# Re-laying a planner's engine orders in a gated-attention plus maxout kernel: load pace, margins, row-tiled groups, head order and filler products

## The chip, the core and the metric

The kernel runs on one core of one Trainium2 chip. The metric is the device time of one execution in microseconds (us); the median of several executions counts. A core has five engines that each run their own instruction list strictly in order: PE (matrix products; its weight loads are shown apart as PEld), DVE, ACT, POOL (element-wise work) and SP, which here only issues the loads from memory. They meet through semaphores: an instruction whose input is not there yet holds up everything behind it on its engine.

## What is computed

For 4 batches and 8 heads of 768 tokens with 48 channels each, a recurrent state is decayed and updated per token, and the result goes through a maxout layer:

```python
for t in range(S):
    state = alpha[:, :, t, :, None] * state + np.einsum('bhd,bhe->bhde', k[:, :, t], v[:, :, t])
    y[:, :, t] = np.einsum('bhd,bhde->bhe', q[:, :, t], state)
...
h1 = x @ w1          # x: y of all heads side by side, 3072 tokens x 384
h2 = x @ w2          # 384 x 1024
g = np.maximum(h1, h2)
return (g @ w_out).astype(np.float32)
```

## The kernel before

**Units.** The tokens are cut into 12 units of 256 tokens (two chunks, a = 0 and 1, of 128). Unit u belongs to batch u % 4, so the state passes from unit u - 4 to unit u. Each unit has an attention part, `gla(u)`, and a maxout part, `moe(u)`.

**The attention part.** One load brings alpha (tile af), six bring k, q and v by chunk (kf, qf, vf). ACT takes the logarithm (lg, L372; two buffers). PE sums it over the tokens in row-tiled products (`e_cs`, L393, called cs below: 4 products that use 64 of the 128 rows each) and forms the decays (`e_de`, L384). ACT then takes three kinds of exponentials (em L403, in place L406, de L409). DVE makes qn (L421) and POOL kn (L418) and casts v to vc (L424). For each chunk PE transposes qn and kn (L435, called tp), DVE copies them out (qk, L437), PE forms k times v (kv, L459) and the scores (`e_p`, L481, called p: 8 products on 48 of 128 rows, in two row halves), DVE masks these (pt, L487), PE forms y from the scores and the carried state (L496 and L499), ACT copies y (yc, L507), PE transposes it (L513, called xt), and DVE copies it to tile xt (L515).

**The maxout part.** max(h1, h2) = h2 + relu(h1 - h2), so the kernel computes relu(x (w1 - w2)) w_out + x (w2 w_out). Four h groups per unit (L534, 6 products each; group f needs the weight quarter w12 number f, made by DVE at L326) are followed by relu (ACT L545, or DVE L542 for group 1) and 22 output products (L562, called o; part of them need w2o = w2 w_out, formed once at L340 to L363 from all the weight quarters). ACT copies the result (L568) and issues the store (L571).

**What sets the order.** Nothing is ordered by hand. Each piece of work is recorded by `Plan.add` with its engine, an assumed duration, an assumed latency until others may use its result (`lat`, else the table `LAT`), and a key. `Plan.schedule` then runs the recorded work through time on all engines at once: whenever an engine is free, the ready piece with the smallest key is taken. The instructions are put out in the order of the starts so found; only this order reaches the chip, and the assumed times do not. So a wrong assumed duration does not make anything slower by itself; it puts pieces into the in-order list of an engine ahead of, or behind, where they would fit. Keys: `gla(u)` has 10u and a little more, `moe(u)` has 10u + `KEY_M`, the preparation of the weights has `KEY_W12`, `KEY_W` and `KEY_WO`. Loads run on SP in the order in which they are recorded: those in the text `HEAD` first (u10 is alpha and chunk 0 of unit 1, u11 its chunk 1, w21 is quarter 1 of w2, and so on), then unit 2, 3 and so on. Input tiles have six buffers.

**Filler products.** `busy` (L351) records products on a zero tile that nobody reads: some with key -10 that stand first on PE, and some with key 1000, which the planner takes only where PE would have nothing else.

Of the kernel before, what the change touches and what calls it, by code (L numbers as in the profile page):

```python
# [13 lines left out]
class Op:  # L14
    __slots__ = ("n", "eng", "fn", "dur", "lat", "key", "deps", "succ", "start", "end", "ps", "w")

# [7 lines left out]
class Plan:  # L24
# [5 lines left out]

    LAT = {"PE": 0.21, "ACT": 0.15, "DVE": 0.14, "POOL": 0.14, "SP": 0.0}

    def __init__(self):
# [6 lines left out]

    def add(self, eng, fn, dur, reads=(), writes=(), key=0.0, lat=None, ps=()):
        o = Op(len(self.ops), eng, fn, dur, self.LAT[eng] if lat is None else lat, key)
        for r in reads:
            if r in self.last_w:
                o.deps.add(self.last_w[r])
            self.readers.setdefault(r, []).append(o.n)
        for w in writes:
            if w in self.last_w:
                o.deps.add(self.last_w[w])
            for r in self.readers.pop(w, ()):  # L50
                if r != o.n:
                    o.deps.add(r)
            self.last_w[w] = o.n
        for x in (*reads, *writes, *ps):
            if x in self.psum and x not in o.ps:
                o.ps.append(x)
                self.psum[x][2] += 1
        o.w = (*writes, *reads)[:1]
        self.ops.append(o)
        return o  # L60

    def schedule(self, caps):
        ops = self.ops
# [11 lines left out]
        free = {e: 0.0 for e in self.LAT}  # L75
# [28 lines left out]

        order, t, n_left = [], 0.0, len(ops)
        while n_left:
            moved = False
            for e in self.LAT:
# [3 lines left out]
                for n in ready[e]:  # L112
                    if ready_at[n] > t + 1e-9:
                        continue
                    o = ops[n]
                    k = (o.key, n)
                    if best is None or k < best[0]:
# [14 lines left out]
                free[e] = t + o.dur  # L132
                order.append(n)
# [25 lines left out]

KEY_W12 = 11  # L160
KEY_W = 12
KEY_WO = 13
KEY_M = 25
HEAD = "u00 u01 w20 w10 wo0 w21 w11 wo1 u10 w22 w12 wo2 u11 w23 w13 wo3"


@with_exitstack
def kernel(
# [18 lines left out]
    nc = tc.nc  # L187
# [106 lines left out]
    def load(u, part=None):  # L294
# [72 lines left out]
    def gla(u):  # L367
# [21 lines left out]
        def e_cs():  # L389
            for r in range(2):  # L390
                for a in range(2):
# [19 lines left out]
        for a in range(2):  # L411
# [65 lines left out]
            def e_p(qk=qk, pp=pp):  # L477
                for j in range(HP):
                    for e in range(2):
# [40 lines left out]
    def moe(u):  # L520
# [26 lines left out]
        for m in range(2):  # L547
# [51 lines left out]
    for u in range(NU):  # L599
        if u + 1 < NU:  # L600
            if u:
                load(u + 1)
            gla(u + 1)
        moe(u)
# [34 lines left out]
```

## Time and profile before

| what | value |
|---|---|
| three timed runs | 155.95, 157.93, 158.33 us; median 157.93 us |
| the profiled execution's own time | 157.39 us |
| its span (first to last instruction) | 155.5 us |
| busy on PE / DVE / ACT / POOL | 139.5 / 95.3 / 78.4 / 66.9 us |
| read from memory / written | 23.59 MB / 4.72 MB |
| first cs product on PE / last product ends | 5.36 us / 151.46 us |

Of the profile of an execution these views are used: the page with the span cut in 40 slices (a digit is the busy share in tenths; PEclk is the granted PE clock), the table of stages (busy time of each engine in a stretch that is chosen by its two times), the timeline of an engine (start, duration, line, output<-input, count, and in brackets how long the engine was idle before it and for what), and the chain of waits that ended last. PE overlaps the products, so the duration of a group of products by itself (some 0.2 to 0.3 us longer than its share) is less telling than the distance from one group's start to the next, or than the chain, which counts each stretch once.

### The profile page before, as it was taken

What the parts mean: (1) busy time and instruction counts of PE and PEld (TensorE: products, weight loads), DVE (VectorE), ACT (ScalarE), POOL (GpSimd) and SP (SyncE); (2) the same over time, 40 slices, a digit from 0 to 9 for tenths busy, and PEclk for the clock granted to TensorE, in tenths of its full rate; (3) what the DMA queues carried; (4) which work ended last, traced back from release to release, by engine and by line L of the source; (5) the groups of instructions that cost most, each with busy time, mean ns of one, the idle gap of its engine ahead of it and who ended that gap; (6) DMA issues with size and microseconds to landing.
All of it is one profiled execution on the core that took longest, in us unless ns stands there. A gap on an engine that the chain in (4) does not pass through costs nothing.

```text
span 155.5 us, 4176 instructions
## 1 busy us (share of the span) xinstructions
PE 139.5 (90%) x1642; PEld 99.0 (64%) x1642; DVE 95.3 (61%) x198; ACT 78.4 (50%) x164; POOL 66.9 (43%) x124
## 2 busy tenths in 40 slices
PE   7955895979999999999896969999999999999990
PEld 7843453556767676756664746766867667677750
DVE  6379627493889889496394476494681965931100
ACT  3603362338775672843925743744936537245430
POOL 7872223622736373471570671652734615500000
PEclk9998699699999999999999999999999999999998
DMA  4999999899999997998997999999911102002202
GB/s 118 221 274 325 278 250 259 254 289 203 239 221 255 232 265 157 287 212 181 267 239 152 188 276 184 294 226 198 261 27 68 40 0 101 4 0 101 100 6 101
DMA packets 94931, 28.58 MB, mean 184 GB/s; under 512 B 87744, under 2 KB 94912, under 8 KB 94912
## 3 DMA queue, kind: packets, MB, share of 16 engines
q1 hardware_dynamic: 91648, 23.60, 67.4%
q10 hardware_dynamic: 3264, 4.72, 8.4%
q8 instruction: 13, 0.21, 0.6%
q14 instruction: 6, 0.05, 0.1%
HBM read 23.59 MB, written 4.72 MB: 182 GB/s over the span
## 4 chain that ended last, share of the span: by engine, by line
SPq 39%; PE 29%; DMA 12%; ACT 6%; issue 4%; DVE 4%; POOL 2%; ACTq 1%; POOLq 0%; DVEq 0%
SPq L308 31%; PE pb L562 16%; DMA af<-in_alpha_dram 7%; SPq L322 6%; PE pb L534 5%; DMA vf<-in_v_dram 3%; PE pb L435 2%; DMA qf<-in_q_dram 2%; SPq L299 2%; ACT em L403 2%; PE pb L481 2%; DVE qn L421 2%; ACT os L568 2%; POOL kn L418 1%; PE pb L499 1%
## 5 line engine op out<-in xcount | busy, mean ns | idle before, releaser
L562 PE MATMUL pb<-wo,gt 128*128 128x384 f16 x192 | 39.9, 327 | 0.1
L534 PE MATMUL pb<-xt,w 128*128 128x256 f16 x288 | 36.0, 272 | 2.3 <-DVE w2T L345 2.1
L487 DVE TENSOR_TENSOR pt<-pb,u 128x512 f16<-128x512 f32 x48 | 30.3, 683 | 5.9 <-PE pb L481 5.6
L418 POOL TENSOR_TENSOR kn<-kf,em 128x384 f16<-128x384 f32 x24 | 23.5, 998 | 17.1 <-ACT em L403 7.6
L534 PEld LDWEIGHTS <-w 128*128 128x128 f16 x288 | 26.7, 97 | 5.8 <-DVE w L326 1.5
L545 ACT ACTIVATE gt<-pb 128x512 f16<-128x512 f32 x36 | 21.4, 598 | 12.9 <-PE pb L534 12.7
L424 POOL CAST vc<-vf 128x384 f16<-128x384 f32 x24 | 12.1, 504 | 33.4 <-DMA vf<-in_v_dram 16.6
L568 ACT COPY os<-pb 128x384 f32<-128x384 f32 x24 | 11.4, 477 | 25.4 <-PE pb L562 25.4
L421 DVE TENSOR_TENSOR qn<-qf,pb 128x384 f16<-128x384 f32 x24 | 12.5, 550 | 17.8 <-ACT pb L406 14.7
L451 POOL TENSOR_TENSOR sb<-tm,dd 64x192 f16<-64x192 f32 x40 | 20.1, 502 | 6.3 <-DVE tm L471 3.9
L562 PEld LDWEIGHTS <-gt 128*128 128x128 f16 x192 | 16.1, 98 | 8.4 <-DVE gt L542 0.5
L437 DVE COPY qk<-pb 128x1024 f16<-128x1024 f16 x24 | 16.0, 682 | 2.6 <-PE pb L435 2.2
L507 ACT CAST yc<-pb 128x384 f16<-128x384 f32 x24 | 11.4, 480 | 12.1 <-PE pb L499 12.1
L515 DVE COPY xt<-pb 128x384 f16<-128x384 f16 x24 | 8.5, 355 | 13.7 <-PE pb L513 8.4
L562 PE MATMUL pb<-w2o,xt 128*128 128x384 f16 x72 | 15.7, 327 | 0.0
L372 ACT ACTIVATE lg<-af 128x768 f16<-128x768 f32 x12 | 10.1, 841 | 9.8 <-DMA af<-in_alpha_dram 9.8
L542 DVE TENSOR_SCALAR gt<-pb 128x512 f16<-128x512 f32 x12 | 8.2, 686 | 10.0 <-PE pb L534 9.9
L481 PE MATMUL pb<-qk 48*128 48x128 f16 x192 | 10.0, 226 | 3.1 <-DVE qk L437 1.8
L403 ACT ACTIVATE em<-pb 128x384 f32<-128x384 f32 x24 | 11.3, 494 | 2.2 <-PE pb L384 1.0
L481 PEld LDWEIGHTS <-qk 48*128 48x128 f16 x192 | 5.7, 97 | 9.2 <-issue 4.3
L471 DVE TENSOR_TENSOR tm<-pb,sb 64x192 f32<-64x192 f32 x32 | 11.2, 351 | 0.6
L499 PE MATMUL pb<-vc,pt 128*128 128x48 f16 x192 | 11.5, 184 | 0.1
(51 smaller groups left out, 176.5 us busy)
## 6 DMA issues: line engine op xcount, KB each, us to landing
af<-in_alpha_dram SPq DMA_DIRECT2D x12, 384.0 KB, 5.1
kf<-in_k_dram SPq DMA_DIRECT2D x24, 192.0 KB, 4.5
qf<-in_q_dram SPq DMA_DIRECT2D x24, 192.0 KB, 4.5
vf<-in_v_dram SPq DMA_DIRECT2D x24, 192.0 KB, 4.4
out_dram<-os ACTq DMA_DIRECT2D x12, 384.0 KB, 3.2
w2f<-in_moe_w_dram SPq DMA_DIRECT2D x4, 384.0 KB, 4.5
w1f<-in_moe_w_dram SPq DMA_DIRECT2D x4, 384.0 KB, 4.8
wof<-in_moe_w_out_dram SPq DMA_DIRECT2D x4, 384.0 KB, 5.5
```

The source lines that it names most:

```text
L308: nc.sync.dma_start(out=T[n][:, a], in_=src[b, :, t0 + 128 * a : t0 + 128 * a + 128, :].rearrange("h p d -> p h d"),)
L403: add("ACT", lambda csv=csv, em=em: nc.scalar.activation(out=EM[em], in_=csv(), func=ACTF.Exp, scale=-1.0), 0.38, reads=[("cs", u, a)], wr ...
L418: add("POOL", lambda a=a, kn=kn, m3=m3: nc.gpsimd.tensor_mul(out=kn[:, :, 0:D], in0=KF[n][:, a], in1=EM[m3]), 0.95, reads=[("kf", n, a), ( ...
L421: add("DVE", lambda a=a, qn=qn: nc.vector.tensor_mul(out=qn[:, :, 0:D], in0=QF[n][:, a], in1=b32(("cs", u, a), DM).rearrange("p (h d) -> p ...
L437: add("DVE", lambda qk=qk, tp=tp: nc.vector.tensor_copy(out=qk, in_=b16(tp, 1024).rearrange("p (w j c) -> p w j c", w=2, j=HP)), 0.6, read ...
L451: add("POOL", lambda r=r, e=e, sb=sb, dd=dd, tmi=tmi: nc.gpsimd.tensor_mul(out=sb[r, :, e], in0=TM[tmi][r], in1=dd[r, :].unsqueeze(2).to_b ...
L481: nc.tensor.matmul(b32(pp[e], 512).rearrange("p (j c) -> p j c", j=HP)[:, j, :], lhsT=qk[r, 1, j, :], rhs=qk[r, 0, j, :], start=True, stop ...
L487: add("DVE", lambda e=e, pt=pt, pp=pp: nc.vector.tensor_mul(out=pt[:, e], in0=b32(pp[e], 512).rearrange("p (j c) -> p j c", j=HP), in1=u16 ...
L534: nc.tensor.matmul(t[:, m, :], lhsT=w12[:, ds, f * 128 : f * 128 + 128], rhs=xt[:, ds].rearrange("p a c -> p (a c)"), start=(ds == 0), sto ...
L545: add("ACT", lambda g2=g2, v2=v2: nc.scalar.activation(out=g2, in_=v2(), func=ACTF.Relu), 0.48, reads=[x], writes=[("gt", u % 3, f2)], key ...
L562: nc.tensor.matmul(b32(x, DM), lhsT=l, rhs=r, start=first and y == 0, stop=last and y == len(ws) - 1)
L568: add("ACT", lambda m=m, x=x: nc.scalar.copy(out=os_[:, m, :], in_=b32(x, DM)), 0.38, reads=[x], writes=[("os", u % 3)], key=k0 + 4 + m)
```

## The change

All edits are to what the planner assumes and to what is recorded; the instructions of the attention and maxout parts are the same, and only their order differs.

```diff
+    PAD = 0.15
+    SWITCH = 0.1
+    STICK = 2.0
...
-        o = Op(len(self.ops), eng, fn, dur, self.LAT[eng] if lat is None else lat, key)
+        o = Op(len(self.ops), eng, fn, dur, self.LAT[eng] + self.PAD if lat is None else lat, key)
+        o.tiled = tiled
...
-                    k = (o.key, n)
+                    k = (o.key - (self.STICK if o.tiled and was_tiled else 0.0), n)
...
+                if e == "PE":
+                    o.dur += self.SWITCH if was_tiled and not o.tiled else 0.0
+                    was_tiled = o.tiled
...
-KEY_W12 = 11
-KEY_W = 12
-KEY_WO = 13
-KEY_M = 25
-HEAD = "u00 u01 w20 w10 wo0 w21 w11 wo1 u10 w22 w12 wo2 u11 w23 w13 wo3"
+KEY_W12 = 5
+KEY_W = 6
+KEY_WO = 10
+KEY_M = 18
+NBUSY = 160
+HEAD = "u00 u01 w20 u10 w10 w21 u11 wo0 w23 wo1 w11 w22 wo3 w12 wo2 w13"
...
-            add("SP", l_a, 1.45, writes=[("af", n)], key=-1, lat=2.0)
+            add("SP", l_a, 1.5, writes=[("af", n)], key=-1, lat=2.5)
...
-                add("SP", l_c, 0.98, writes=[(nm, n, a)], key=-1, lat=2.0)
+                add("SP", l_c, 0.99, writes=[(nm, n, a)], key=-1, lat=2.5)
...
-        add("SP", lambda: nc.sync.dma_start(out=dst, in_=src), 1.1, writes=[(f"w{m}f", g)], key=-1, lat=2.0)
+        add("SP", lambda: nc.sync.dma_start(out=dst, in_=src), 1.2, writes=[(f"w{m}f", g)], key=-1, lat=2.5)
...
-        add("PE", e_cs, 0.42, reads=[("lg", lgi), "t2"], writes=[("cs", u, 0), ("cs", u, 1)], key=k0)
+        add("PE", e_cs, 0.35, reads=[("lg", lgi), "t2"], writes=[("cs", u, 0), ("cs", u, 1)], key=k0, tiled=True)
...
-            add("PE", e_p, 0.36, reads=[("qk", m3)], writes=pp, key=kk)
+            add("PE", e_p, 0.27, reads=[("qk", m3)], writes=pp, key=kk, tiled=True)
...
-            0.06, reads=[("os", u % 3)], key=k0 + 6, lat=3.0)
+            0.06, reads=[("os", u % 3)], writes=[("out", u)], key=k0 + 6, lat=2.0)
+        add("SP", lambda: None, 1.06, writes=[("out", u)], key=-2)
...
-    busy(30, -10)
-    busy(60, 1000)
+    busy(34, -10)
+    busy(NBUSY, 1000)
+    add("SP", lambda: None, 0.6, key=-3)
```

So the planner now takes 0.15 us more for every handoff, a little more for each load, and a stretch of 1.06 us on the load queue for every store (no instruction stands behind it: it only delays the assumed loads). After a row-tiled piece another row-tiled piece is preferred, and leaving one costs 0.1 us. The recorded filler products go from 90 to 194. Lines after the edits are 8 higher than in the listing of before (L351 is then L359, L534 is L542, L571 is L579).

Three places of the orders that follow. **ACT, middle of the kernel** (around unit 6; af_69 and lg_93 belong to unit 6, af_70 and lg_94 to unit 7, em_106 is written by the first exponential of unit 6 in the list, de_113 the last of unit 5). Before:

```order
L409 ACTIVATE de_113<-pb_62 128x16
L372 ACTIVATE lg_93<-af_69 128x8x2x48
L545 ACTIVATE gt_141<-pb_66 128x512
L545 ACTIVATE gt_141<-pb_64 128x512
L507 CAST yc_136<-pb_61 128x384
L568 COPY os_144<-pb_62 128x384
L507 CAST yc_135<-pb_61 128x384
L372 ACTIVATE lg_94<-af_70 128x8x2x48
L568 COPY os_144<-pb_68 128x384
L403 ACTIVATE em_106<-pb_61 128x384
```

Now, from the same de_113 on, first to the exponentials of unit 6:

```order
L417 ACTIVATE de_113<-pb_67 128x16
L380 ACTIVATE lg_93<-af_69 128x8x2x48
L576 COPY os_144<-pb_68 128x384
L579 DMA out_dram<-os_144 128x2x384
L553 ACTIVATE gt_142<-pb_64 128x512
L411 ACTIVATE em_106<-pb_68 128x384
```

and at the end of those exponentials:

```order
L515 CAST yc_136<-pb_67 128x384
L414 ACTIVATE pb_64<-pb_64 128x384
L417 ACTIVATE de_114<-pb_64 128x16
L380 ACTIVATE lg_94<-af_70 128x8x2x48
L576 COPY os_145<-pb_63 128x384
```

The logarithm of unit 7 stood ahead of the exponentials of unit 6; it now stands behind them. The logarithms of units 8 and 9 moved in the same way (unit 8's stands ahead of the small last exponential only).

**SP, the head.** From the last load of unit 0 on, before:

```order
L308 DMA vf_87<-in_v_dram 128x8x48
L322 DMA w2f_147<-in_moe_w_dram 128x3x256
L322 DMA w1f_148<-in_moe_w_dram 128x3x256
L322 DMA wof_149<-in_moe_w_out_dram 128x2x384
L322 DMA w2f_147<-in_moe_w_dram 128x3x256
L322 DMA w1f_148<-in_moe_w_dram 128x3x256
L322 DMA wof_149<-in_moe_w_out_dram 128x2x384
L299 DMA af_70<-in_alpha_dram 128x8x96
```

Now:

```order
L316 DMA vf_87<-in_v_dram 128x8x48
L330 DMA w2f_147<-in_moe_w_dram 128x3x256
L307 DMA af_70<-in_alpha_dram 128x8x96
L316 DMA kf_76<-in_k_dram 128x8x48
L316 DMA qf_82<-in_q_dram 128x8x48
L316 DMA vf_88<-in_v_dram 128x8x48
L330 DMA w1f_148<-in_moe_w_dram 128x3x256
L330 DMA w2f_147<-in_moe_w_dram 128x3x256
```

Unit 1 comes ahead of most weights. In both orders the head is 26 loads of the same sizes in all; the last is a quarter of w_out before and quarter 3 of w1 now, and from the 27th load on (alpha of unit 2) the queue is the same.

**PE, the row-tiled pieces in the middle.** qk are the operands of p, lg those of cs. Before, around the end of a p:

```order
L481 LDWEIGHTS qk0_129
L481 MATMUL pb2_63<-qk0_129 128x128
L481 LDWEIGHTS qk0_129
L481 MATMUL pb0_61<-qk0_129 128x128
L562 LDWEIGHTS xt0_137
L562 MATMUL pb6_67<-w2o0_154,xt0_137 128x384
```

Now, around the end of the second p of a unit:

```order
L489 LDWEIGHTS qk0_129
L489 MATMUL pb0_61<-qk0_129 128x128
L489 LDWEIGHTS qk0_129
L489 MATMUL pb6_67<-qk0_129 128x128
L401 LDWEIGHTS t20_157
L401 MATMUL pb7_68<-lg0_93,t20_157 128x384
```

In six units the second p is now followed by cs of the next unit, with no full-height product between. Counted over all of PE's list from cs of unit 2 to the end, a row-tiled piece is left for another kind 30 times before and 24 times now. Up to that same cs, PE's list has 24 h products, 12 o products, 28 y products and 9 xt products before; now 42, 8, 40 and 12. All products of w2o stand ahead of it in both; so does the attention of units 0 and 1, but for the y and xt of unit 1's second chunk, which before come behind it.

Fillers on PE: 45 ahead of cs of unit 0, 42 and 3 behind it before; 62 ahead of it, 96 between it and cs of unit 1, and 36 after that now, the last of them ahead of the first h product.

More of the change, by code (lines that the diff above doesn't have):

```diff
@@ L14 @@
 class Op:
-    __slots__ = ("n", "eng", "fn", "dur", "lat", "key", "deps", "succ", "start", "end", "ps", "w")
+    __slots__ = ("n", "eng", "fn", "dur", "lat", "key", "deps", "succ", "start", "end", "ps", "w", "tiled")
     def __init__(self, n, eng, fn, dur, lat, key):
@@ L39, in ps, with add @@
         self.psum[name] = [banks, group, 0, None]
-    def add(self, eng, fn, dur, reads=(), writes=(), key=0.0, lat=None, ps=()):
-        o = Op(len(self.ops), eng, fn, dur, self.LAT[eng] if lat is None else lat, key)
+    def add(self, eng, fn, dur, reads=(), writes=(), key=0.0, lat=None, ps=(), tiled=False):
+        o = Op(len(self.ops), eng, fn, dur, self.LAT[eng] + self.PAD if lat is None else lat, key)
+        o.tiled = tiled
         for r in reads:
@@ L103, in place @@
             return got
-        order, t, n_left = [], 0.0, len(ops)
+        order, t, n_left, was_tiled = [], 0.0, len(ops), False
         while n_left:
@@ L130, in schedule @@
                 ready[e].remove(n)
+                if e == "PE":
+                    o.dur += self.SWITCH if was_tiled and not o.tiled else 0.0
+                    was_tiled = o.tiled
                 o.start, o.end = t, t + o.dur
-                free[e] = t + o.dur
+                free[e] = o.end
                 order.append(n)
@@ L600 @@
         if u + 1 < NU:
-            if u:
+            if f"u{u + 1}0" not in HEAD:
                 load(u + 1)
```

## Prediction

> **What bounds the kernel now.** I read the page first, then the clock, then a table of stages, then the timelines of the engines around the holes that it shows.
>
> ```profile
> PE 139.5 (90%) x1642; PEld 99.0 (64%) x1642; DVE 95.3 (61%) x198; ACT 78.4 (50%) x164; POOL 66.9 (43%) x124
> PEclk9998699699999999999999999999999999999998
> DMA  4999999899999997998997999999911102002202
> ```
>
> PE is busy 90% of the span, but the load queue is full too until about slice 29 (113 us). The clock dips twice, near 16 and 28 us (rival 1). Which of PE and the loads rules is seen from stages that I cut at the start of cs of each unit; shown are those of units 4, 5, 6, 7, 8, 10 and 11, the last one up to the end of the last product. The columns are length, then busy time and instructions of PE, PEld, DVE, ACT, POOL, then granted clock, DMA share and GB/s. The last row sums all ten stages, from cs of unit 2 at 36.43 us on.
>
> ```profile
> 52.40:62.69 10.29, 10.29 (x147) 7.37 (x147) 8.75 (x19) 6.31 (x14) 5.75 (x11) 1.00 1.00 225
> 62.69:73.56 10.87, 10.58 (x134) 7.53 (x133) 7.70 (x16) 6.07 (x13) 5.67 (x11) 1.00 0.99 230
> 73.56:86.11 12.55, 10.70 (x129) 7.19 (x128) 7.13 (x15) 6.60 (x14) 5.38 (x11) 1.00 1.01 219
> 86.11:97.77 11.66, 10.36 (x130) 7.41 (x130) 7.28 (x16) 6.16 (x13) 5.87 (x12) 1.00 1.01 220
> 97.77:108.07 10.30, 10.13 (x126) 7.30 (x126) 6.61 (x13) 6.12 (x14) 5.53 (x11) 1.00 1.09 245
> 118.26:128.53 10.27, 10.12 (x125) 7.26 (x126) 6.46 (x13) 5.50 (x13) 4.27 (x8) 1.00 0.11 41
> 128.53:151.46 22.93, 22.80 (x218) 16.12 (x216) 8.44 (x17) 10.76 (x23) 4.27 (x8) 1.00 0.14 53
> sum 115.03, PE 111.05 PEld 78.39 DVE 72.75 ACT 64.14 POOL 50.17; mean PE 11.10 PEld 7.84 DVE 7.27 ACT 6.41 POOL 5.02
> ```
>
> From cs of unit 2 (36.43 us) to the last product (151.46 us) PE has 111.05 us of work in 115.03 us. So 3.98 us are holes, most of them between 73 and 98 us. A unit costs PE about 10.3 us. The loads are faster:
>
> ```profile
> 60.84 0.58 SPq L299 DMA_DIRECT2D af<-in_alpha_dram  x1
> 102.41 0.83 SPq L299 DMA_DIRECT2D af<-in_alpha_dram  x1
> ```
>
> These are the alpha loads of units 6 and 11: 41.57 us for five units, 8.3 us each. From unit 2 on the loads gain 2 us per unit on PE, so the end is set by PE: when it gets to cs of unit 2, how much work is then left, and the holes. What made the holes:
>
> ```profile
> 73.89 0.84 ACT L372 ACTIVATE lg<-af 128x768 f16<-128x768 f32 x1 [1.39 <-DMA af<-in_alpha_dram]
> 83.38 0.84 ACT L372 ACTIVATE lg<-af 128x768 f16<-128x768 f32 x1 [3.45 <-DMA af<-in_alpha_dram]
> 91.78 0.84 ACT L372 ACTIVATE lg<-af 128x768 f16<-128x768 f32 x1 [1.88 <-DMA af<-in_alpha_dram]
> ...
> 77.15 0.40 PE L435 MATMUL pb<-ident,qn 128*128 128x128 f16 x4 [0.53 <-DVE qn L421]
> 85.02 0.34 PE L513 MATMUL pb<-ident,yc 128*128 128x128 f16 x3 [1.19 <-ACT yc L507]
> 93.16 0.40 PE L481 MATMUL pb<-qk 48*128 48x128 f16 x8 [1.30 <-ACT gt L545]
> ```
>
> The logarithms of units 7, 8 and 9 stand so early in ACT's list that ACT waits for alpha, 1.39, 3.45 and 1.88 us, though their results are wanted only at cs of these units (86.11, 97.77, 108.07 us). What stands behind them (exponentials, yc, relu) is late, and PE waits 0.53 + 1.19 + 1.30 = 3.02 us of the 3.98.
>
> **Term 1, the middle: holes.** The planner now assumes later loads and counts the stores, and the logarithms of units 7 to 9 have moved behind the exponentials of the unit before. They will be reached some 4 us after cs of units 6, 7 and 8. Counted in the new list with the durations below, PE has 34, 44 and 55 us of work from cs of unit 2 (35 us) to these, so they start near 70, 80 and 91 us with a hole of about 1 us, so ACT asks for alpha at about 74, 84 and 95 us; the rows say that it landed at 73.9, 83.4 and 91.8. The waits of 1.4 to 3.5 us shrink to some tenths. What then comes late is little: 0.96 us of other holes stay. New ones can come near units 3 to 5, where the loads have hardly a lead and PE arrives earlier than before; I add 0.3. Holes: 1.3 us, at best 0.3 (the last two stages have 0.28 together), at worst the old 3.98.
>
> **Term 2, the head: when cs of unit 2 starts, and what is done by then.**
>
> ```profile
> 36.43 0.61 PE L393 MATMUL pb<-lg,t 64*128 64x384 f16 x4
> ...
> 32.32 0.83 POOL L330 CAST wo<-wof 128x768 f16<-128x768 f32 x1 [2.35 <-DMA wof<-in_moe_w_out_dram]
> ...
> 33.52 0.84 ACT L372 ACTIVATE lg<-af 128x768 f16<-128x768 f32 x1 [0.20 <-DMA af<-in_alpha_dram]
> ...
> 32.99 0.96 DVE L326 TENSOR_TENSOR w<-w1f,w2f 128x768 f16<-128x768 f32 x1
> ```
>
> The head loads the same 26 tiles in both orders, and its last one landed at 32.3 us (the POOL row had waited for it). Now w1's quarter 3 has that place: DVE makes w12 of it by 32.3 + 1.0 = 33.3. The one ahead, a quarter of w_out, lands about 1 us sooner; cast, it is ready at 32.1, and 12 products of w2o follow, 12 x 0.162 = 1.95 us: 34.1. Then the last h group of unit 0 (0.66), and cs of unit 2: 34.8, with handoffs 35.1 us. It cannot be before the logarithm of unit 2 is done, 33.52 + 0.84 = 34.4; as a late bound I take the 36.4 of now.
>
> PE has also done more by then: by the lists 18 h, 12 y and 3 xt products more, and 4 o products fewer. Durations of one come from the chain of waits, where the pieces stand back to back:
>
> ```profile
> 112.80 0.33 PE pb L481 x8
> 113.13 0.59 PE pb L562 x3
> ...
> 138.04 0.17 PE pb L513 x3
> ...
> 139.03 2.62 PE pb L534 x24
> 141.65 3.57 PE pb L562 x22
> ...
> 151.46 0.48 ACT os L568
> ```
>
> An h product is 2.62 / 24 = 0.109, an o product 3.57 / 22 = 0.162, an xt product 0.17 / 3 = 0.055 us; the 12 y products of a chunk took 0.37 us by their starts:
>
> ```profile
> 136.49 0.21 PE L496 MATMUL pb<-sb,qk 128*128 128x96 f16 x1
> ...
> 136.86 0.48 PE L562 MATMUL pb<-wo,gt 128*128 128x384 f16 x2
> ```
>
> So 18 x 0.109 + 0.37 + 3 x 0.055 - 4 x 0.162 = 1.85, rounded to 1.9 us, less is left behind cs of unit 2. That is possible since PE stood half empty there (two rows below), while the first h groups of unit 1 now fit in.
>
> **Term 3, row-tiled pieces.** Three o products right behind a p took 0.59 us instead of 3 x 0.162 = 0.49: leaving a row-tiled piece costs 0.10 us. It happens 24 times instead of 30 from cs of unit 2 on: 0.6 us less. Bounds 0 and 0.6.
>
> **Term 4, fillers, at nothing.**
>
> ```profile
> 1.05 4.29 PE L351 MATMUL pb<-wsrc 128*128 128x128 f16 x45 [1.05 <-DVE wsrc L250]
> 6.01 2.50 PE L351 MATMUL pb<-wsrc 128*128 128x128 f16 x42
> ```
>
> A filler takes 0.06 us, the first ones 0.095. 17 more ahead of cs of unit 0 push it back by 1.0 to 1.6 us (from 5.36), since they stand ahead in a strict list, and the next 48 push the transposes back by as much again. What hides it: nothing of unit 0 is wanted before the second quarter of w1 lands, about 26 us; PE's own rows show it waiting at 11 to 15 us. Were that cover gone, the 1.6 us would go onto cs of unit 2, which the bound of 36.4 holds. Margins and the stores' stretch on SP put out no instruction.
>
> **Sum.** 35.1 (cs of unit 2) + 111.05 - 1.9 - 0.6 = 108.55 of work + 1.3 of holes = 144.95, the last product. Behind it stand the copy, the store and its landing, 155.5 - 151.46 = 4.04, and outside the span 157.39 - 155.5 = 1.89. Together 150.9 us, against 157.39 of the profiled execution, which lies 0.5 under the median of the three runs (157.93; 155.95 to 158.33). I expect the new median at 150.9, 4.5% under the old one. With all best ends: 34.4 + 108.5 + 0.3 + 4.04 + 1.89 = 149.1.
>
> **Rival 1, the clock halves once more at a bad time.**
>
> ```profile
> 11.00:14.50 3.50, 2.00 (x29) 1.51 (x29) 3.26 (x8) 1.21 (x2) 0.88 (x3) 1.00 0.98 310
> 14.50:18.20 3.70, 3.20 (x21) 1.72 (x22) 3.46 (x6) 0.83 (x1) 1.26 (x2) 0.54 1.09 333
> ...
> 24.80:28.20 3.40, 1.42 (x19) 1.16 (x17) 3.20 (x6) 0.00 (x0) 1.66 (x2) 1.00 0.87 181
> 28.20:32.00 3.80, 3.80 (x27) 2.19 (x25) 1.78 (x4) 1.43 (x2) 1.63 (x4) 0.55 1.00 318
> ```
>
> Twice a stretch of 3.5 us with PE busy 57% and 42% is followed by as long a stretch at half clock. The new list has fillers until the first h group, about 19 us, and none after; from there to the second quarter of w1, about 27 us, PE has 6 us of work for 8. If that share again halves the clock, the stretch of 3.4 us would fall on 28 to 32 us or on 31 to 35, and at the worst half of it, 1.7 us, goes onto cs of unit 2: 152.6 us. Speaking against it is that 6 of 8 is more than either share in the rows. The Trainium skill (TensorE: Matmul & The Clock Gate, Part 1: The HAM clock gate) says that the clock falls to half after one idle window of about 3.4 us and rises after a busy one; the lengths agree with the trace (both slow stretches are about 3.4 us), but the rows show that half a window of idleness is enough. By that rule alone, with no window wholly idle, this rival would not occur.
>
> **Rival 2, the plan does not come true.** The margins are guesses, and if the logarithms still meet late loads (at 84 us the margin is only 0.5 us), the 3.98 us of holes stay: 35.1 + 108.55 + 3.98 + 4.04 + 1.89 = 153.6; with cs of unit 2 at 36.4 as well, 154.9. For it: ACT's list has its logarithms of units 3 to 5 as tightly as before. Against it: the lead of the loads grows by 2 us per unit.
>
> **Rival 3, slower: a handoff that is late in every unit.** In the new steady order y of the second chunk follows its p after cs, 12 h products, the first y and de: 0.43 + 0.10 + 1.31 + 0.37 + 0.2 = 2.4 us, in which DVE must mask both halves (2 x 0.64 us), with other copies queued ahead. If DVE is late, PE stands still with all its o products behind the waiting y. From 0.65 us per unit over the ten units left the gain is gone; at 1.0 us it is 150.9 + 10 = 160.9. For it: DVE is busy 8.75 of 10.29 us in the stage from 52.40. Against it: in the later stages DVE has 6.5 to 7.7 of 10.3, the same pieces per unit, and PE had no holes with 11 o products, y and 2 more between that p and its y: 11 x 0.162 + 0.37 + 0.32 = 2.5 us.
>
> **How the numbers follow.** Forecast 60%, rival 1 13%, rival 2 19%, rival 3 8%. About 2% is what a measurement of this kernel can tell from no change; 2% under 157.93 is 154.8. The forecast, rival 1 and half of rival 2 lie below: 82%. Half of rival 2 and a weak rival 3 are within: 12%. Slower by over 2%: 6%. The range runs from the best ends, 149.1 and a little for shorter handoffs, to the far end of rival 2: 148.8 to 155.0.
>
> **What would show it.** Right: cs of unit 2 near 35 us; the logarithms of units 7 to 9 wait under 1 us each; PE idle from there to its last product under 1.5 us; stages of 10.1 to 10.3 us from unit 4 on; one maxout part alone at the end, with no other change in the last 4 us. Wrong: alpha landing later than now (the load pace changed), a clock digit under 9 between 28 and 36 us (rival 1), ACT rows with waits for alpha of over 1 us (rival 2), or PE waiting for pt in each stage (rival 3).

## The result, and the profile after

The change takes 148.5 us in the median of four executions (147.72 to 149.33), the kernel before 157.4 us beside it on the same chip. The ratio is 0.946, with a 95% interval of 0.937 to 0.956: 5.4% faster. The forecast was 150.9 us (4.5% under its median of 157.93), its range 148.8 to 155.0. The direction is right. The median of 148.5 lies 0.3 us under the low end of that range, but the kernel before also ran 0.5 us faster here than in the three runs that the forecast started from; as a share, 5.4% lies between the 4.5% of the forecast and the 5.8% of its low end. Some executions of any kernel here are some per cent slower than the rest; ratios here and below leave out those over 1.5% above the fastest of their kernel.

The page of the profiled execution (149.33 us, span 147.3 us), the same three lines that were shown of before:

```profile
PE 139.4 (95%) x1746; PEld 105.7 (72%) x1746; DVE 96.2 (65%) x198; ACT 77.9 (53%) x164; POOL 66.8 (45%) x124
PEclk9999999599999999999999999999999999999999
DMA  4998969997999999969999999999999420030202
```

PE is busy for the same 139.4 us (before 139.5), 104 more filler products included, in a span that is 8.2 us shorter. One dip of the clock is left, in slice 8, near 27 us. The loads end in slice 32 (118 us).

The table of stages, cut at cs of a unit as before (the same columns; units 2, 4, 5, 6, 7, 8 and the last, then the sum of all ten):

```profile
37.70:45.26 7.56, 7.56 (x84) 4.78 (x85) 4.23 (x9) 4.81 (x11) 4.07 (x7) 1.00 1.08 243
...
53.67:64.37 10.70, 10.70 (x143) 7.87 (x141) 8.64 (x19) 6.61 (x15) 5.19 (x10) 1.00 0.93 208
64.37:72.09 7.72, 7.72 (x100) 5.33 (x100) 4.82 (x11) 4.88 (x11) 5.23 (x10) 1.00 0.99 210
72.09:82.00 9.91, 9.91 (x135) 7.49 (x130) 8.14 (x17) 5.85 (x13) 5.79 (x11) 1.00 1.02 225
82.00:92.28 10.28, 10.28 (x147) 7.93 (x142) 8.18 (x17) 5.98 (x14) 5.22 (x10) 1.00 1.01 229
92.28:102.02 9.74, 9.74 (x132) 7.39 (x127) 7.24 (x14) 5.95 (x14) 5.76 (x11) 1.00 1.06 243
...
121.12:143.31 22.19, 22.17 (x240) 16.14 (x234) 10.16 (x20) 10.39 (x22) 4.32 (x8) 1.00 0.11 39
sum 105.61, PE 105.59 PEld 77.72 DVE 71.89 ACT 61.57 POOL 50.12; mean PE 10.56 PEld 7.77 DVE 7.19 ACT 6.16 POOL 5.01
```

From cs of unit 2 on PE is busy for 105.59 of 105.61 us; it was 111.05 of 115.03. Two things are to be seen. The holes are gone altogether, as far as the profile shows idle time. And PE's *busy* time fell by 5.5 us, though the same instructions stand behind cs of unit 2 but for some 1.9 us of them: busy time is not work.

**What busy time hides.** I therefore took every product of PE from cs of unit 2 on, the distance from its start to the start of the next one, and compared it with the median distance of its kind in the kernel before (0.109 us for h, 0.162 for o, 0.056 for a transpose, and so on). What a distance has over its median is put down to the place where it stands.

| us, from cs of unit 2 to the last product's end | before | change |
|---|---|---|
| all products at the median distance of their kind | 104.0 | 102.2 |
| over it, at the steps where a wait is shown (shown as idle) | 5.7 (3.9) | 0 (0) |
| over it, at the edges of row-tiled pieces | 6.4 | 5.1 |
| over it, at the edges of other pieces | 0.3 | 0.2 |
| inside a piece (negative, since the four cs products lie two by two) | -1.4 | -1.9 |
| sum | 115.0 | 105.6 |

So the 9.4 us are 1.8 of work done earlier, 5.7 of holes, 1.3 at row-tiled edges and 0.6 in the two last rows. Before had 11 steps with a shown wait; each lasted 0.16 us (1.8 / 11) longer than is shown as idle, since the profile's end of the product ahead, which is modelled, lies that much inside the wait. Against the 9.4 stands cs of unit 2, at 37.70 us instead of 36.43.

**ACT in the middle.** The logarithms of units 6, 7 and 8 in ACT's timeline, and the issue of alpha of unit 7 in SP's:

```profile
69.30 0.84 ACT L380 ACTIVATE lg<-af 128x768 f16<-128x768 f32 x1 [1.85 <-DMA af<-in_alpha_dram]
77.72 0.84 ACT L380 ACTIVATE lg<-af 128x768 f16<-128x768 f32 x1 [1.44 <-DMA af<-in_alpha_dram]
86.11 0.84 ACT L380 ACTIVATE lg<-af 128x768 f16<-128x768 f32 x1
```

```profile
72.70 1.58 SPq L307 DMA_DIRECT2D af<-in_alpha_dram  x1
```

ACT still stands 1.85 and 1.44 us for alpha of units 6 and 7, and alpha of unit 7 came at 77.7 us instead of 73.9, its issue at 72.70 instead of 68.52. But PE shows no idle time for it: there is other work in its list just then.

**The head.** Three timelines (POOL, DVE, PE) around cs of unit 2, and the stretches in front of it by windows:

```profile
33.63 0.83 POOL L338 CAST wo<-wof 128x768 f16<-128x768 f32 x1 [2.61 <-DMA wof<-in_moe_w_out_dram]
```

```profile
34.60 0.96 DVE L334 TENSOR_TENSOR w<-w1f,w2f 128x768 f16<-128x768 f32 x1
```

```profile
35.00 2.11 PE L367 MATMUL pb<-wo,w2T 128*128 128x384 f16 x12
36.95 0.82 PE L542 MATMUL pb<-xt,w 128*128 128x256 f16 x6
37.70 0.50 PE L401 MATMUL pb<-lg,t 64*128 64x384 f16 x4
```

```profile
22.09:25.50 3.41, 2.04 (x37) 1.52 (x38) 3.38 (x8) 0.67 (x2) 2.27 (x4) 1.00 0.95 320
25.50:28.91 3.41, 3.41 (x19) 2.13 (x18) 2.32 (x6) 0.54 (x1) 0.83 (x1) 0.50 0.96 311
...
25.37:37.70 12.33, 12.33 (x102) 8.69 (x100) 7.42 (x12) 5.52 (x10) 2.48 (x3) 0.86 0.96 283
```

The last quarter of w_out landed at 33.63 us and was cast by 34.46 (the prediction had it landed near 31.3 and cast by 32.1); the last quarter of w12 was made from 34.60 to 35.56. The order of pieces in front of cs is the predicted one (12 products of w2o, the last h group, cs), 2.6 us later. But PE did not wait for these weights. It has no gap from 25.37 us on, and by the distances its pieces from there to 37.70 are 10.5 us at their medians; 1.7 us more lie in the window of 3.41 us that ran at half clock, and 0.2 at edges. It came to the 12 products at 35.00 straight from 18 h products. Ahead of 25.37 us PE waits for DVE (four waits of 0.25 to 0.53 us from 22 us on), which is busy for 3.38 of the 3.41 us of the window from 22.09.

**The end.** The chain of waits ends with one maxout part alone:

```profile
137.10 2.62 PE pb L542 x24
139.72 3.59 PE pb L570 x22
```

Before it ended with two of them, one behind the other; the second stands in the last two rows here, the first in the prediction's rows from 139.03 us on:

```profile
145.22 2.62 PE pb L534 x24
147.84 3.59 PE pb L562 x22
```

This moves work, and does not save any: from the last product to the end of the span it is 4.0 us in both.

### The profile page after: what moved, and what is told of

The parts are those of the page before. It is cut to its first block, busy times and chain, and to the rows that moved or that the text cites. A ratio compares the mean times of both kernels' runs of the same rounds, so it can differ in the third digit from the quotient of the medians.

```text
span 147.3 us, 4387 instructions
## 1 busy us (share of the span) xinstructions
PE 139.4 (95%) x1746; PEld 105.7 (72%) x1746; DVE 96.2 (65%) x198; ACT 77.9 (53%) x164; POOL 66.8 (45%) x124
## 4 chain that ended last, share of the span: by engine, by line
PE 81%; SPq 8%; DMA 4%; DVE 3%; issue 1%; ACT 0%
PE pb L570 30%; PE pb L542 23%; SPq L316 7%; PE pb L443 6%; PE pb L489 5%; DMA w1f<-in_moe_w_dram 4%; PE pb L367 3%; PE pb L507 3%; PE pb L521 3%; PE pb L401 3%; PE pb L504 2%; PE pb L467 2%; PE pb L392 2%; DVE qk L445 1%; DVE pt L495 1%
## 5 line engine op out<-in xcount | busy, mean ns | idle before, releaser
L570 PE MATMUL pb<-wo,gt 128*128 128x384 f16 x192 | 38.6, 328 | 0.0
L542 PE MATMUL pb<-xt,w 128*128 128x256 f16 x288 | 37.3, 273 | 1.3 <-DVE w L334 1.3
L542 PEld LDWEIGHTS <-w 128*128 128x128 f16 x288 | 25.9, 98 | 7.3 <-issue 1.9
L570 PEld LDWEIGHTS <-gt 128*128 128x128 f16 x192 | 17.1, 98 | 8.4
L445 DVE COPY qk<-pb 128x1024 f16<-128x1024 f16 x24 | 16.6, 690 | 9.6 <-PE pb L443 7.4
L429 DVE TENSOR_TENSOR qn<-qf,pb 128x384 f16<-128x384 f32 x24 | 13.0, 551 | 14.3 <-ACT de L417 5.0
L359 PE MATMUL pb<-wsrc 128*128 128x128 f16 x194 | 14.5, 237 | 1.1 <-DVE wsrc L258 1.1
L380 ACT ACTIVATE lg<-af 128x768 f16<-128x768 f32 x12 | 10.1, 842 | 8.3 <-DMA af<-in_alpha_dram 8.1
L359 PEld LDWEIGHTS <-wsrc 128*128 128x128 f16 x194 | 13.0, 108 | 1.3 <-DVE wsrc L258 1.1
L414 ACT ACTIVATE pb<-pb 128x384 f32<-128x384 f32 x24 | 11.5, 499 | 0.0
```

The source lines that it names most:

```text
L359: add("PE", lambda: nc.tensor.matmul(bank("wq0")[:, 384:512], lhsT=wsrc[:, 0:128], rhs=wsrc[:, 0:128], start=True, stop=True), 0.107 if ke ...
L429: add("DVE", lambda a=a, qn=qn: nc.vector.tensor_mul(out=qn[:, :, 0:D], in0=QF[n][:, a], in1=b32(("cs", u, a), DM).rearrange("p (h d) -> p ...
L445: add("DVE", lambda qk=qk, tp=tp: nc.vector.tensor_copy(out=qk, in_=b16(tp, 1024).rearrange("p (w j c) -> p w j c", w=2, j=HP)), 0.6, read ...
L542: nc.tensor.matmul(t[:, m, :], lhsT=w12[:, ds, f * 128 : f * 128 + 128], rhs=xt[:, ds].rearrange("p a c -> p (a c)"), start=(ds == 0), sto ...
L570: nc.tensor.matmul(b32(x, DM), lhsT=l, rhs=r, start=first and y == 0, stop=last and y == len(ws) - 1)
```

## The experiments

Theory, as it stood ahead of the runs: the gain is the holes of the middle, which the logarithms standing too early on ACT made, and it comes with the assumed pace of the loads; the keys and the head only do their small part. Rivals: the head order and the keys carry it; or the margins do; or the row-tiled preference. "Vs before" and "vs change" say which kernel was edited. All of them compute the whole result.

| run | ratio to before (95%) | cs of unit 2 | from there to the end of the last product | idle shown in it | over, at waits | over, row-tiled |
|---|---|---|---|---|---|---|
| before | 1 | 36.43 | 115.0 | 3.94 | 5.7 | 6.4 |
| the change | 0.946 (0.937–0.956) | 37.70 | 105.6 | 0.00 | 0 | 5.1 |
| e1_pace | 0.970 (0.962–0.978) | 38.76 | 108.4 | 0.29 | 1.1 | 5.8 |
| e2_ln_late | 0.998 (0.993–1.004) | 35.52 | 116.2 | 4.97 | 6.7 | 6.5 |
| e3_no_pace | 0.966 (0.957–0.975) | 36.70 | 108.8 | 1.99 | 3.0 | 4.7 |
| e4_fill90 | 0.944 (0.935–0.953) | 37.02 | 105.5 | 0.00 | 0 | 5.1 |
| e5_no_pad | 0.959 (0.953–0.964) | 38.24 | 106.6 | 0.05 | 0.2 | 5.6 |
| e6_no_tiled | 0.949 (0.938–0.961) | 37.40 | 106.8 | 0.46 | 1.0 | 5.1 |
| e7_head | 0.986 (0.978–0.995) | 37.31 | 112.0 | 2.03 | 4.0 | 6.0 |
| e8_no_keys | 0.961 (0.953–0.969) | 38.27 | 107.5 | 1.29 | 2.0 | 5.1 |
| e9_ln_behind_relu | 0.988 (0.982–0.995) | 36.76 | 113.4 | 2.13 | 3.9 | 6.5 |
| e10_pace_pad | 0.965 (0.958–0.972) | 36.47 | 108.5 | 0.49 | 0.8 | 6.2 |
| e11_paired_p | 0.951 (0.943–0.959) | 37.50 | 105.8 | 0.45 | 1.1 | 4.3 |
| e12_pad_double | 0.963 (0.956–0.971) | 37.08 | 108.0 | 1.87 | 2.2 | 4.9 |

Columns three to seven are us of one profiled execution each, the last two by the distances between starts. The ratio of each run is to the kernel before timed beside it.

**e1_pace** (vs before): the load pace alone.

```diff
-            add("SP", l_a, 1.45, writes=[("af", n)], key=-1, lat=2.0)
+            add("SP", l_a, 1.5, writes=[("af", n)], key=-1, lat=2.5)
...
-            0.06, reads=[("os", u % 3)], key=k0 + 6, lat=3.0)
+            0.06, reads=[("os", u % 3)], writes=[("out", u)], key=k0 + 6, lat=2.0)
+        add("SP", lambda: None, 1.06, writes=[("out", u)], key=-2)
...
+    add("SP", lambda: None, 0.6, key=-3)
```

The other loads go to 0.99 and 1.2 us, 2.5 us of latency, as in the change.

> The kernel before with one thing of the change: the assumed load pace (1.5, 0.99 and 1.2 us, latency 2.5), the 0.6 us at the start of SP and the stretch of 1.06 us per store. In its list the logarithms of units 7 to 9 stand behind the exponentials of the unit before, as in the change; keys, head, margins, row-tiled preference and fillers are as before. Theory (the holes between 73 and 98 us came from logarithms that stood too early, and the pace alone moves them): the 3 us of shown holes go, ratio to before 0.975 to 0.982, and PE's shown waits from cs of unit 2 on fall from 3.9 us to under 1. Rival (the margins at handoffs and the new head are what removed the waits): ratio 0.99 to 1.00, other waits of 2 to 4 us in their place.

Measured: 3.0% faster. Its stages of units 6 and 7, and the sum, in the table of stages:

```profile
73.70:84.40 10.70, 10.52 (x131) 7.39 (x132) 7.43 (x16) 6.02 (x14) 5.77 (x11) 1.00 1.09 244
84.40:94.40 10.00, 10.00 (x125) 7.13 (x124) 7.08 (x15) 5.86 (x13) 5.18 (x10) 1.00 1.02 226
...
sum 108.41, PE 108.12 PEld 78.17 DVE 71.72 ACT 62.86 POOL 49.42; mean PE 10.81 PEld 7.82 DVE 7.17 ACT 6.29 POOL 4.94
```

These two stages took 12.55 and 11.66 us before. A few assumed durations that no instruction carries give more than half of the whole gain. Most of the edit is the stretch for the store: by the old numbers the planner loads a unit in 1.45 + 6 x 0.98 = 7.3 us, by the new ones in 1.5 + 6 x 0.99 + 1.06 = 8.5, and the chip took 8.3 (alpha to alpha, before).

**e2_ln_late** (vs before): the logarithms of units 7 to 9 moved on ACT behind the last exponential of the unit before, nothing else.

```diff
+    lns = [o for o in P.ops if o.eng == "ACT" and o.w[0][0] == "lg"]
+    des = [o for o in P.ops if o.eng == "ACT" and o.w[0][0] == "de"]
+    for u in (7, 8, 9):
+        lns[u].start = max(lns[u].start, des[u - 1].start + 1e-6)
```

> The kernel before with its order kept, but for three instructions: the logarithms of units 7, 8 and 9 are moved on ACT behind the last exponential of the unit before. Theory (they block ACT while alpha is not there): 3 us less, ratio 0.978 to 0.983, and no wait of ACT for alpha of over 1 us from 70 us on. Rival (ACT would have been late anyway, or the wait reappears in qn, kn or vc, which wait for their own loads): ratio 0.99 to 1.00.

Measured: no difference. PE's and ACT's timelines, and two stages:

```profile
79.80 0.33 PE L459 MATMUL pb<-vc,kn 128*128 128x96 f16 x4 [0.66 <-ACT gt L545]
...
90.88 0.33 PE L459 MATMUL pb<-vc,kn 128*128 128x96 f16 x4 [0.61 <-ACT gt L545]
```

```profile
78.42 0.83 ACT L372 ACTIVATE lg<-af 128x768 f16<-128x768 f32 x1
79.16 0.59 ACT L545 ACTIVATE gt<-pb 128x512 f16<-128x512 f32 x1
```

```profile
51.60:63.76 12.16, 10.46 (x147) 7.30 (x147) 8.79 (x19) 6.32 (x14) 5.78 (x11) 1.00 0.93 207
...
75.22:86.24 11.02, 10.36 (x129) 7.28 (x129) 7.30 (x15) 6.16 (x13) 5.25 (x10) 1.00 0.96 215
```

The logarithm now waits for nothing (78.42), but the relu that stands behind it (79.16) is what PE's next piece wants: PE waits 0.66 us at 79.80. The stage of unit 6 fell from 12.55 to 11.02 us, and the three stages that the edit touches are 33.2 us together instead of 34.5. Others grew in this execution: that of unit 4 is 12.16 instead of 10.29, with 1.7 us of holes, in which DVE waited 1.85 us for a load of q; all lists up to there are those of before, so the edit did not make this hole. One profiled execution can therefore not tell the three stages' 1.3 us from chance; the median of the executions, which shows no gain, is what counts. So the theory in its simple form, "the place of three logarithms", is not borne out.

**e9_ln_behind_relu** (vs before): the same three behind two more relus.

```diff
+    gts = sorted(o.start for o in P.ops if o.eng == "ACT" and o.w[0][0] == "gt")
+    for u in (7, 8, 9):
+        lns[u].start = [s for s in gts if s > des[u - 1].start][1] + 1e-6
```

> As e2_ln_late, but the logarithms of units 7 to 9 go one step further back on ACT, behind the two relu pieces that follow the last exponential; nothing else of the order before is touched. Theory (the early logarithms did cause the holes of 73 to 98 us, and e2 only put 0.8 us of logarithm ahead of the relu that frees the bank for the second kv): those stages fall to 10.3 to 10.6 us each, ratio to before 0.978 to 0.986. Rival (each place in that list has some piece that is late, so single moves gain nothing; the whole list must be laid anew): 0.992 to 1.00, with waits of 0.5 us and more at another place in each unit.

Measured: 1.2% faster, between what the theory and its rival gave. The stages of units 6, 7 and 8, and ACT's timeline:

```profile
74.44:85.20 10.76, 10.45 (x129) 7.27 (x129) 7.23 (x15) 6.16 (x13) 5.24 (x10) 1.00 0.99 220
85.20:95.49 10.29, 10.29 (x130) 7.32 (x130) 7.21 (x16) 6.17 (x13) 5.66 (x11) 1.00 1.04 233
95.49:106.77 11.28, 10.41 (x125) 7.30 (x125) 6.72 (x13) 6.95 (x15) 5.64 (x11) 1.00 0.98 222
```

```profile
99.60 0.84 ACT L372 ACTIVATE lg<-af 128x768 f16<-128x768 f32 x1 [0.76 <-DMA af<-in_alpha_dram]
```

Units 6 and 7 gain 12.55 + 11.66 - 10.76 - 10.29 = 3.2 us, close to the 3.0 that the prediction read from the rows. In the next stage 0.98 us (11.28 for 10.30) goes back: ACT now asks for the next alpha too early (0.76 us), and PE waits 0.67 us for the relu behind it. Moved by hand, a wait goes on to the next unit; laid anew as a whole (e1) it does not.

**e3_no_pace** (vs change): the reverse of e1.

> The change with the old load pace, without the stretches for the stores and the start. Its list has the logarithms of units 7 to 11 ahead of the exponentials again. Theory (pace): the waits for alpha return in the middle, 2 to 4 us of holes on PE from cs of unit 2 on, ratio to before 0.965 to 0.975 (change: 0.946). Rival (margins and head carry the gain): ratio 0.945 to 0.952 and no holes.

Measured: 0.966, with 1.99 us of idle PE again. ACT and PE:

```profile
74.10 0.84 ACT L380 ACTIVATE lg<-af 128x768 f16<-128x768 f32 x1 [1.69 <-DMA af<-in_alpha_dram]
...
75.22 0.59 ACT L553 ACTIVATE gt<-pb 128x512 f16<-128x512 f32 x1
...
81.86 0.84 ACT L380 ACTIVATE lg<-af 128x768 f16<-128x768 f32 x1 [3.58 <-DMA af<-in_alpha_dram]
```

```profile
75.86 0.22 PE L504 MATMUL pb<-sb,qk 128*128 128x96 f16 x1 [1.04 <-ACT gt L553]
```

The long waits for alpha are back, and behind the one that ends at 74.10 the relu of 75.22 is late, for which PE waits 1.04 us. The longest of them (3.58 us) costs PE little: 0.30 and 0.17 us of idle right behind it. Taking the pace out costs about 2 points, putting it in alone brings 3.

**e7_head** (vs before): the order of the loads alone.

```diff
-HEAD = "u00 u01 w20 w10 wo0 w21 w11 wo1 u10 w22 w12 wo2 u11 w23 w13 wo3"
+HEAD = "u00 u01 w20 u10 w10 w21 u11 wo0 w23 wo1 w11 w22 wo3 w12 wo2 w13"
...
-            if u:
+            if f"u{u + 1}0" not in HEAD:
```

> The kernel before with the new head order alone (unit 1 loaded ahead of most weights). Theory (the head changes what PE has done by cs of unit 2, not when it comes): cs of unit 2 within 1.5 us of before, 1 to 2 us more of work done by then, the holes of the middle as before: ratio 0.985 to 0.995. Rival A (the head is the main gain): ratio under 0.975. Rival B (the last weights become later and hold everything): over 1.00.

Measured: 1.4% faster. The holes of the middle did not stay as they were, which I had expected: 2.03 us of idle PE are left of 3.94. cs of unit 2 is later than before (37.31), and the rest is 3.0 us shorter: 1.7 of it at waits, 0.5 is work done earlier, the remaining 0.8 lies at edges and inside pieces.

**e8_no_keys** (vs change): KEY_W12, KEY_W, KEY_WO, KEY_M back to 11, 12, 13, 25.

> The change with the four old keys (weights later, maxout part later against the attention of the units ahead). Theory (keys matter little once the pace is right, since the list keeps its logarithms behind the exponentials): ratio 0.945 to 0.955. Rival (the new priority of the maxout part is what keeps PE full): 0.960 or more, with holes on PE in the middle.

Measured: 0.961, by the middle of the interval 1.5 points over the change (the intervals overlap a little), with 1.29 us of idle, such as this one in PE's timeline:

```profile
91.97 0.20 PE L504 MATMUL pb<-sb,qk 128*128 128x96 f16 x1 [0.73 <-POOL sb L459]
```

I had held the keys to be nearly free; most likely they are not. That the maxout parts which they bring forward are PE's stock of work is how I read it; no run moves these parts alone.

**e5_no_pad, e12_pad_double, e10_pace_pad**: the margin. `PAD = 0.15` to 0.0 and to 0.3 in the change; and e1 with `LAT` raised by 0.15 on before.

> The change with PAD = 0 (handoffs assumed as short as before); all else as in the change, replanned. The logarithms of units 7 to 9 stay behind the exponentials. Theory (the margins close the short waits at handoffs, which the busy time hides, and the pace closes the long ones): 1 to 2.5 us more than the change behind cs of unit 2, short waits at transposes, kv and y on PE; ratio to before 0.950 to 0.962. Rival (margins only shuffle the order): 0.942 to 0.949, no wait on PE behind cs of unit 2.

> The change with PAD = 0.3 instead of 0.15. Theory (margins work by closing short waits, and with 0.15 none is left on PE behind cs of unit 2, so more gives nothing): 0.942 to 0.952, no shown wait there. Rival (larger margins move the logarithms of units 8 and 9 ahead of the exponentials again, and ACT waits for alpha): 0.955 or more.

> The kernel before with the load pace of e1 and the longer handoffs (0.15 us more), with old head, keys, fillers and no row-tiled preference. Theory (pace and margins carry the part behind cs of unit 2, the head the part ahead of it): behind cs of unit 2 some 106.5 to 108 us (before 115.0, e1 108.4, change 105.6), ratio 0.958 to 0.970. Rival (margins do nothing on their own): as e1, 0.970 or more.

Measured: 0.959, 0.963 and 0.965. Without the margin hardly any wait is shown, but the work between cs of unit 2 and the end takes 1.0 us longer in small steps, and cs is 0.5 us later; the intervals overlap a little, so this is the likely reading, not a sure one. With the margin doubled I had expected no more and no less than the change, and it is 1.7 points slower. The list is another one again, with logarithms of units 8 and 9 ahead of exponentials, but these wait for nothing (84.88 and 93.15 us). The one large hole in PE is elsewhere:

```profile
69.66 0.34 PE L467 MATMUL pb<-vc,kn 128*128 128x96 f16 x4 [1.61 <-POOL kn L426]
```

PE waits here for kn of POOL, and POOL had stood 2.88 us for a load of v (its cast starts at 67.19). On before, margin and pace together (0.965) are not better than the pace (0.970) by more than the intervals. The parts do not add up: each gives the planner another list, and 0.15 has no property of its own that the runs show.

**e6_no_tiled** (vs change): `SWITCH` and `STICK` to 0, durations of cs and p back to 0.42 and 0.36. **e11_paired_p** (vs change): the first p of a unit waits in the plan for the second qk, so both p stand together.

```diff
+    for u, ((p0, q0), (p1, q1)) in pairs.items():
+        if u >= 2:
+            p0.deps.add(q1)
```

> The change without the row-tiled preference: SWITCH and STICK 0 and the old durations of cs and p. Theory (entering and leaving a row-tiled piece costs PE 0.1 us each; the preference saves some six of each): 0.6 to 1.3 us more than the change, ratio to before 0.948 to 0.956. Rival (the preference costs order elsewhere and gives nothing): 0.940 to 0.947.

> The change, with the planner made to hold the first p of a unit from unit 2 on until the second is ready too, so that a row-tiled piece is left 20 instead of 24 times behind cs of unit 2. Theory (each entry and exit costs 0.1 us): 0.8 us less than the change, ratio 0.938 to 0.944. Rival (the later first p makes y late and opens holes): 0.950 or more.

Measured: 0.949 and 0.951, both not to be told from the change; for e11 I had expected a gain of 0.2 to 0.8 points. Without the preference PE leaves a row-tiled piece 24 times, as often as with it; the six fewer came with the rest of the re-laying. With p in pairs it is 20 times and 0.8 us are saved there (5.1 to 4.3), as the price per edge says, but 1.1 us of new holes take them back.

**e4_fill90** (vs change): 104 fillers left out when the instructions are put out (45, 42 and 3 are kept, as before has), all else in the same order.

```diff
+        seen, keep = [0], [45, 42, 3]
...
+                if o.w == ("wsrc",):
+                    done += 1
+                    if len(seen) > len(keep) or done > keep[len(seen) - 1]:
+                        continue
```

> The change with its order kept, and only 90 fillers as before (45 ahead of cs of unit 0, 42 behind it, 3 after kv; the other 104 left out; nobody reads them). Theory (fillers buy nothing but a full clock later): unit 0 starts 1 us sooner, the clock is halved more often between 15 and 35 us, and what falls after 25 us, where PE is dense, costs up to 1.7 us: ratio 0.945 to 0.957. Rival A (the halved clock was the larger part of what the head lost before): 3 us more than the change, ratio 0.965. Rival B (fillers only delay real work): 1 us less than the change, ratio 0.940.

Measured: 0.944, no difference. The clock did answer, in windows ahead of 27.5 us:

```profile
13.90:17.30 3.40, 3.32 (x44) 2.57 (x42) 2.06 (x5) 2.58 (x5) 0.00 (x0) 0.50 0.92 229
17.30:20.70 3.40, 1.47 (x18) 1.07 (x16) 2.67 (x5) 1.95 (x6) 2.45 (x4) 1.00 1.06 259
20.70:27.50 6.80, 6.15 (x58) 4.26 (x55) 5.52 (x11) 1.74 (x3) 4.00 (x6) 0.50 0.98 304
```

Three windows at half clock instead of one, and yet cs of unit 2 comes at 37.02 us, not later. Until 25.4 us PE waits for DVE in both runs, and the products of w2o start at 25.36 us here and at 25.37 in the change. Behind that point this run has 2.2 us at half clock, the change 3.4.

## Why the prediction was right or wrong

- **What bounds the kernel** (PE from cs of unit 2 on, not the loads): right. The end follows PE's list in every run, and the loads end 25 us ahead of the last product.
- **Term 1, holes** ("the waits of 1.4 to 3.5 us shrink to some tenths", 3.98 to 1.3 us): right that the early logarithms make holes and that these go with the new pace (e9, e1, e3); mis-sized, and wrong in how. The holes were 5.7 us, not 3.98, because busy time covers the start of each, and nothing of them is left. The step that failed is "alpha landed at 73.9, 83.4": I took the landing times of before for the change, and alpha of unit 7 came 3.8 us later, so ACT's waits stayed (1.85 and 1.44 us). They cost nothing that is shown, because the order leaves PE other work in those moments. Why the load queue ran later was not tried. It did so in two steps: in the head one kf issue of unit 2 took 4.33 us, and vf of that unit was issued 2.3 us later than before; alpha of unit 3 was 1.7 us later, that of unit 5 2.6, that of unit 6 4.4.
- **Term 2, head** (cs of unit 2 at 35.1, 1.9 us done by then): the 1.9 is right (1.8), the time is 2.6 us late and outside the bounds (34.4 to 36.4). The step that failed is the path: I put cs behind the landing of the last quarter of w_out, with PE half empty until then. PE was busy without a gap from 25.37 us on, with 10.5 us of work up to cs, 1.7 us more at half clock and 0.2 at edges, and this set the 37.70. The landing was wrong too ("lands about 1 us sooner; ready at 32.1": landed at 33.63, cast by 34.46), since I let the loads keep the landing times of their places in the list; but PE reached the 12 products only at 35.00, so this cost at most 0.06 us. Without the half clock cs would have come near 36.0, still 0.9 us late.
- **Term 3, row-tiled pieces** (0.6 us): 1.3 measured. The price of leaving was nearly right (0.10, measured 0.12); entering costs about as much, which I had not looked for. The planner's preference for row-tiled neighbours does not bring it: without it there are 24 leavings too (e6).
- **Term 4, fillers at nothing**: right (e4). The cover is of the kind that was named: PE waits in the head until 25.4 us, with the 104 fillers and without them.
- **Rival 1, the clock**: it occurred in the profiled execution, at 25.5 to 28.9 us, and only there: the other three executions had a mean clock of 0.997 to 0.999 and took 147.72 to 148.56 us, against 0.988 and 149.33. So it is worth 0.8 to 1.6 us, as priced (at most 1.7; 1.7 by the distances). I gave it 13%, and that it fell into the profiled execution is chance. Nor does the share that I named decide it: the window ahead of the dip had PE busy for 2.04 of 3.41 us (60%), the one ahead of that for 1.92 (57%), and only the first of these was followed by half clock (more in the last section). By the rule of the Trainium skill (TensorE: Matmul & The Clock Gate, Part 1: The HAM clock gate) it takes one idle window of about 3.4 us, and the dip would not have occurred. This trace does not agree, since no window ahead of the dip was idle.
- **Rival 2, the plan does not come true**: its condition came (ACT waits 1.44 us for alpha of unit 7), its price did not, see term 1. **Rival 3, p to y**: did not occur; from cs of unit 2 on PE shows no wait for pt.
- **Sum**: cs of unit 2 +2.6, work and holes 105.6 instead of 109.85, outside the span +0.1: 149.3 for 150.9. That 149.3 lies so near to 150.9 is partly luck: two errors of opposite sign, cs 2.6 us too early and the rest 4.2 us too long. The larger one is that idle time was read off busy time. With 5.7 for the holes and 1.3 at the edges, the low end would have been some 2.4 us lower (1.7 + 0.7).
- **Signs**: two of five "right" ones came (PE idle under 1.5 us; one maxout part alone at the end). cs of unit 2 was not near 35 us, the logarithm of unit 7 waited over 1 us, and the stages are not 10.1 to 10.3 us long (10.70, 7.72, 9.91, 10.28), since cs now stands at other places among the products. Of the "wrong" ones three came: alpha landed later, the clock dipped in slice 8, and ACT waited over 1 us.

What stays open: why the loads of units 3 to 7 landed later, and whether margins under or over 0.15 are better by themselves or only by the list that happened. The same doubt stands over the pace in part. Each of the three lists that were laid anew from before (e1, e7, e10) is faster than before, and no run lays one anew for no reason; so how much of the 3.0% is the better pace, and how much any other list would have brought, is not shown. What speaks for the pace is that taking it out (e3) brings the waits for alpha back, at a cost of 2 points.

## What to carry to other kernels

Where a planner lays in-order lists, give it the measured pace of the slowest feeder, stretches for the stores included: durations that no instruction carries were worth 3% here, while moving three misplaced instructions by hand brought 0 and 1.2%. Read idle time from start to start rather than from busy time, since each wait on PE was 0.16 us longer here than it is shown. Before putting a late piece down to a late load, see whether the engine that wants it had run out of other work. When loads are put in another order, their landing times must be worked out anew, for the middle as well; those of the old order were wrong by 2.3 and 3.8 us here.

## What the runs showed of the hardware

**Row-tiled edges cost on both sides.** PE's timeline of the change, where transposes, p, h and cs follow each other:

```profile
107.33 0.39 PE L443 MATMUL pb<-ident,kn 128*128 128x128 f16 x4
107.56 1.46 PE L570 MATMUL pb<-wo,gt 128*128 128x384 f16 x8
...
109.08 0.39 PE L443 MATMUL pb<-ident,kn 128*128 128x128 f16 x4
109.40 0.40 PE L489 MATMUL pb<-qk 48*128 48x128 f16 x8
109.73 1.48 PE L542 MATMUL pb<-xt,w 128*128 128x256 f16 x12
111.15 0.40 PE L489 MATMUL pb<-qk 48*128 48x128 f16 x8
111.38 0.49 PE L401 MATMUL pb<-lg,t 64*128 64x384 f16 x4
```

Four transposes take 0.23 us up to an o product (107.33 to 107.56) and 0.32 up to a p (109.08 to 109.40): 0.09 to enter. A p takes 0.33 us up to an h product (109.40 to 109.73) and 0.23 up to a cs, which is row-tiled too (111.15 to 111.38): 0.10 to leave. Over all edges of the change the means are 0.09 and 0.12 us.

**Half clock after a window that is not idle.** Windows of 3.4 us with PE busy 60% (the change), 43% (e4) and 57% and 42% (before) were each followed by one at half clock; no window was wholly idle. Busy time does not tell which windows these are: in the change one with 57% was followed by full clock, in e6 one with 48%. Work does so better. I counted PE's products in every window at full clock ahead of 42 us in all 14 profiles, each at the median distance of its kind. Of the 16 windows with less than 42% of such work 15 were followed by half clock (23% to 42%; the one that was not, in e10, had 37%), and of those with more than 42% none (the nearest had 42.1% and 42.5%). The line at 42% is an estimate from these windows alone.
